# Regrouping in a fused GFNet mixing and SoLU kernel: one quarter of each transfer becomes a ScalarE copy

## The chip, the cores and the metric

The kernel runs on one core of a Trainium2 chip, in fp32. The metric is the device time of one execution in microseconds (us), as the median of several runs. The core's engines are named as in the profile: PE is TensorE (matmuls; PEld is its weight loads), DVE is VectorE, ACT is ScalarE, POOL is GpSimd, and SP is the engine that only issues transfers. "ACTq" and "SPq" mark work of an engine's sequencer, such as issuing a DMA.

## The reference

```python
def _attn_ref(x, filt_r, filt_i):            # x: 8 x 3136 x 256
    X = np.fft.rfft(x, axis=1)
    F = (filt_r + 1j * filt_i)[None, :, :]
    y = np.fft.irfft(X * F, n=x.shape[1], axis=1)
    return y.astype(np.float32)

def _moe_ref(x, w_in, w_out, g_ln):          # x: 25088 tokens x 256, d_ff 1024
    h = x @ w_in
    e = np.exp(h - np.max(h, axis=-1, keepdims=True))
    sm = e / (np.sum(e, axis=-1, keepdims=True) + 1e-09)
    solu = h * sm
    mu = np.mean(solu, axis=-1, keepdims=True)
    var = np.mean((solu - mu) ** 2, axis=-1, keepdims=True)
    ln = (solu - mu) / np.sqrt(var + 1e-06) * g_ln
    return ln @ w_out
```

The output of the first, with batch and sequence joined, is the input of the second.

## The kernel before, in words

The Fourier part works on one batch element after the other, as matmuls with tables (`first`, `forward`, `multiply`, `inverse`, `back_halves`), with intermediate results in DRAM (`d1`, `d2`). Its result lies in `y`, with channels on partitions, for two elements at a time. Element 0 is done ahead of the main loop; the others are spread over the main loop by the table `PLAN`.

The main loop is `step(k)`, for 196 blocks of 128 tokens and nine more steps (`LAG = 9`). An even step and the odd one after it (pair `j = k // 2`) belong together. Nothing is reordered afterwards: the kernel is recorded under a manual schedule, so the order in which `step` calls its helpers is the order of instructions on every engine.

For one pair of blocks, in the order of the data:
- `product(j, m)` (L867 to L876, matmuls `m<-w_in_sb,...`): the product with `w_in` for a pair of blocks in seven half-size products instead of eight (Strassen's form, Winograd's variant). Products 1, 6, 5 and 3 build up in one PSUM bank; `keep` (L896) copies what the bank holds by then to `h` on ScalarE, and `finish` (L907, L910) adds another bank on VectorE and takes the running minimum `nmax`. Product 3 adds to the bank which the `keep` behind product 5 reads, so it comes after that `keep`.
- `exponential` (L920, ScalarE), `normalize` (L932, VectorE: `h * e`) and `square` (L940, ScalarE, for the variance).
- `turn` (L950, VectorE): a transpose in blocks of 32 x 32. Four blocks of tokens share one `turn` tile `[128, 32, 4, 32]`. Its partition `32 a + j` holds features `32 f + j` of the tokens `32 a` to `32 a + 31` of each block.
- `regroup(p, i)` (L953 to L967): makes from one quarter `a = 2 * (p % 2) + i` of the turned tile the tile `solu_t`, in which all 128 partitions hold features. Partitions `32 a` to `32 a + 31` are read, and for each `q` of 0 to 3 the features with `f % 4 == q` go to the partitions `32 q` to `32 q + 31`: 32 partitions x 8 runs of 128 elements, 128 KB. Both calls of a pair stand in the even step, and their transfers are issued by SP. In the very last pairs a few are issued by ACT and POOL.
- `project_sums` (POOL, L854) and `project(p, m)` (L1022, matmuls `o<-w_out_sb,...`): the product with `w_out`, again in seven half-size products; `keep_out` (L1038, ScalarE) and `finish_out` (L1042, VectorE) join them into `ot` and scale by the token's `rs_t`, and `store_out` writes `ot`.

In an even step ScalarE's order around the change is: `keep_out` (L1038); in every other pair the copy of `rs_t` (L989); loads that belong to the Fourier part where there are any (`spectrum_loads`, L320 `t<-d` and L835 `de<-de_tbl`, issued on ACT's queue); then, in the odd step, `keep` behind product 5 (L896), `keep_out`, `exponential`, `keep_out`, `square`. TensorE's order there is: `project(p, 3)`, `project(p, 4)`, products 7 and 5, `project` 1 and 2, products 3 and 4, `project` 6 and 7.

`solu_t` has two buffers for each `i`; the tile of pair `p` takes the buffer of pair `p - 2`.

Of the kernel before, what the change touches and what calls it, by code (L numbers as in the profile page):

```python
# [110 lines left out]
def kernel(  # L111
# [10 lines left out]
    nc = tc.nc  # L122
# [356 lines left out]
    with ExitStack() as st:  # L479
# [140 lines left out]
        for i, h in [(i, h) for i in range(pieces - 2) for h in range(2)] + [  # L620
# [6 lines left out]
                           in_=ps.rearrange("p (a t c) -> p a t c", t=2, c=P))  # L627
# [36 lines left out]
        for i0, n, rows in ((0, 4, P), (4, 4, P), (8, NP - 9, P), (NP - 1, 1, NQ)):  # L664
            f, at = filters[i0]
            nc.sync.dma_start(
                out=f_dram[i0:i0 + n].rearrange("i u q k c -> (u q) i (k c)")[0:rows],
                in_=f[0:rows, at:at + n].rearrange("p i k c -> p i (k c)"))
# [163 lines left out]
    def load_de(sp, u, dma=nc.scalar.dma_start):  # L832
# [6 lines left out]
    turns, variances, solu_ts, solu_sums, spreads, rss, pos, ots, places, regrouped = (  # L839
        {} for _ in range(10))  # L840
# [112 lines left out]
    def regroup(p, i, dma=nc.sync.dma_start, parts=range(4)):  # L953


        g, second = divmod(p, 2)
        turned = turns[g].rearrange("p (k q) b i -> p k q (b i)", q=4)
        a = 2 * second + i
        if (p, i) not in regrouped:
            if p == last[-1]:  # L960
                st = pools["r"].tile([P, KF, P], FP32, name=f"solu_t_{p}_{i}", tag="r")
            else:
                st = upool.tile([P, KF, P], FP32, name=f"solu_t_{p}_{i}", tag=f"solu_t{i}")
            regrouped[p, i] = st
            solu_ts[p, i] = st[:, 0:KF // 2, :], st[:, KF // 2:KF, :]
        for q in parts:
            dma(out=regrouped[p, i][32 * q:32 * q + 32, :, :], in_=turned[32 * a:32 * a + 32, :, q, :])  # L967

    def least_variance(g):

# [95 lines left out]
    for e in range(1, B):  # L1066
# [5 lines left out]
        for i, t in enumerate(first_at):  # L1072
            if e == 1 and i < EARLY:
                continue
            dma = nc.gpsimd.dma_start
# [23 lines left out]
        for i, t in enumerate(spectrum_at):  # L1099
# [4 lines left out]
            dma = nc.sync.dma_start if e == 1 and t < 8 else nc.scalar.dma_start  # L1104
# [41 lines left out]
    def step(k):  # L1146
# [33 lines left out]
        if not odd:  # L1180
# [41 lines left out]
            if 0 <= j - 3 < pairs - 2:  # L1222
                regroup(j - 3, 0)
                regroup(j - 3, 1)
            elif j - 3 == pairs - 2:
                regroup(j - 3, 1, nc.scalar.dma_start, range(2))
                regroup(j - 3, 0)
                regroup(j - 3, 1, parts=range(2, 4))
                regroup(j - 2, 0)
                regroup(j - 2, 1, parts=range(2))  # L1230
# [107 lines left out]
```

## Time and profile before

| | us |
|---|---|
| median of 3 runs | 1560.1 (1558.52 to 1560.6) |
| profiled execution | 1558.44 |
| its span | 1556.7 |
| PE busy in the span | 1534.5 |
| DVE, POOL, ACT busy | 1241.3, 1107.3, 923.3 |
| granted clock of TensorE | 0.997 |

Times in the profile's rows are from the span's start. Matmuls overlap their weight loads, and their ends are modelled. A number in brackets behind a row of the timeline is the engine's idle time ahead of it and what ended it. Until about 1160 us the Fourier part runs among the token blocks; after that there are token blocks alone.

### The profile page before, as it was taken

The page shows a single profiled execution, that of the slowest core. Times are in us where ns is not written, and L with a number is a line of the kernel's source. Part 1 is how long each engine was busy: PE and PEld are TensorE (multiplying, and loading weights), DVE is VectorE, ACT ScalarE, POOL GpSimd, SP SyncE. Part 2 cuts the span into 40 slices and gives each one's busy share as a digit, 9 for nine tenths or more (in the row PEclk, how much of TensorE's full clock was granted, in tenths as well). Part 3 has the DMA queues.
Part 4 walks back from the last instruction along what each step waited for, and adds up shares of the span by engine and source line. Part 5 has one row for each costly group of instructions (what it writes and reads, how often), then busy time and mean ns, then how long its engine had stood idle before and what let it go on. Part 6 is the DMA issues. An engine that isn't in the chain of part 4 may idle for free. (4 is left out here: it accounts for less than half of the span.)

```text
span 1556.7 us, 36704 instructions
## 1 busy us (share of the span) xinstructions
PE 1534.5 (99%) x12922; PEld 1066.0 (68%) x12922; DVE 1241.3 (80%) x2220; ACT 923.3 (59%) x1893; POOL 1107.3 (71%) x1290
## 2 busy tenths in 40 slices
PE   9999999999999999999999999999999999999997
PEld 6735676666666776667666776667676777777777
DVE  5888878988988798868897699877987777777772
ACT  4556565665556565665656555665656656666662
POOL 2226776797879776986689678996767766676665
PEclk9999999999999999999999999999999999999999
DMA  9779587867986788667886678766874544344444
GB/s 250 267 254 274 160 229 218 238 196 212 245 242 188 188 247 238 198 164 202 248 230 183 166 209 246 209 181 185 228 206 118 135 122 121 97 119 105 107 109 109
DMA packets 340831, 297.58 MB, mean 191 GB/s; under 512 B 27313, under 2 KB 310731, under 8 KB 340649
## 3 DMA queue, kind: packets, MB, share of 16 engines
q1 hardware_dynamic: 277864, 175.33, 42.4%
q0 software_dynamic: 29152, 87.33, 18.7%
q10 hardware_dynamic: 33634, 32.58, 7.1%
q8 instruction: 105, 1.72, 0.5%
q14 instruction: 76, 0.62, 0.1%
HBM read 117.53 MB, written 74.84 MB: 124 GB/s over the span
## 5 line engine op out<-in xcount | busy, mean ns | idle before, releaser
L1022 PEld LDWEIGHTS o<-w_out_sb,solu_t 128*128 128x128 f32 x3136 | 381.7, 192 | 49.9 <-issue 43.1
L1022 PE MATMUL o<-w_out_sb,solu_t 128*128 128x128 f32 x3136 | 401.3, 276 | 3.7 <-DVE ot L1042 3.1
L1022 PEld LDWEIGHTS o<-w_out_sb,u 128*128 128x128 f32 x2352 | 307.3, 192 | 138.3 <-issue 108.6
L875 PE MATMUL m<-w_in_sb,s 128*128 128x512 f32 x760 | 384.5, 607 | 2.4 <-ACT h L896 1.6
L1022 PE MATMUL o<-w_out_sb,u 128*128 128x128 f32 x2352 | 310.7, 276 | 2.3 <-POOL u L854 1.8
L932 DVE SCALAR_TENSOR_TENSOR h<-e,h 128x1024 f32<-128x1024 f32 x196 | 304.5, 1554 | 0.0
L875 PE MATMUL m<-w_in_sb,y 128*128 128x512 f32 x570 | 297.1, 603 | 1.7 <-DVE h L907 1.2
L1038 ACT ACTIVATE ot<-o,rs_t 128x128 f32<-128x128 f32 x392 | 143.2, 367 | 244.6 <-PE o L1022 242.8
L896 ACT COPY h<-m 128x512 f32<-128x512 f32 x285 | 167.7, 588 | 200.5 <-PE m L875 179.7
L854 POOL TENSOR_TENSOR u<-solu_t 128x512 f32<-128x512 f32 x98 | 135.2, 1380 | 186.7 <-DMA solu_t<-turn 131.0
L910 DVE CUSTOM_DVE_ANT_0 h<-m,h 128x512 f32<-128x512 f32 x190 | 130.1, 685 | 166.8 <-ACT h L896 104.0
L940 ACT ACTIVATE h<-h,nmu 128x1024 f32<-128x1024 f32 x196 | 224.9, 1147 | 41.8 <-DVE turn L950 41.7
L950 DVE STREAM_TRANSPOSE turn<-h 128x1024 f32<-128x1024 f32 x196 | 243.2, 1241 | 3.2
L920 ACT ACTIVATE e<-h,nmax 128x1024 f32<-128x1024 f32 x196 | 225.3, 1149 | 9.3 <-DVE h L932 7.9
L854 POOL TENSOR_TENSOR u<-solu_t,u 128x512 f32<-128x512 f32 x98 | 136.9, 1396 | 99.6 <-PE o L1022 99.3
L1042 DVE SCALAR_TENSOR_TENSOR ot<-o,rs_t,ot 128x128 f32<-128x128 f32 x299 | 103.8, 347 | 100.1 <-ACT ot L1038 61.4
L875 PEld LDWEIGHTS m<-w_in_sb,s 128*128 128x128 f32 x760 | 124.5, 191 | 80.3 <-issue 63.0
L854 POOL TENSOR_TENSOR u<-u,solu_t 128x512 f32<-128x512 f32 x98 | 162.6, 1659 | 16.8 <-PE o L1022 7.6
L854 POOL TENSOR_TENSOR solu_t<-solu_t,solu_t 128x512 f32<-128x512 f32 x98 | 155.6, 1587 | 0.9
L875 PEld LDWEIGHTS m<-w_in_sb,y 128*128 128x128 f32 x570 | 93.6, 190 | 89.6 <-issue 45.9
L854 POOL TENSOR_TENSOR s<-y 128x128 f32<-128x128 f32 x190 | 94.4, 497 | 0.5
L437 PEld LDWEIGHTS py<-wb_t,t 50*64 50x64 f32 x3584 | 57.6, 134 | 42.9 <-issue 19.4
(153 smaller groups left out, 1939.0 us busy)
## 6 DMA issues: line engine op xcount, KB each, us to landing
solu_t<-turn SPq DMA_DIRECT2D x780, 128.0 KB
out_dram<-ot SPq DMA_DIRECT2D x196, 128.0 KB
t<-d POOLq DMA_DIRECT2D x112, 200.0 KB, 6.7
t<-d ACTq DMA_DIRECT2D x37, 512.0 KB
f<-f_dram POOLq DMA_DIRECT2D x37, 512.0 KB, 7.9
d<-g POOLq DMA_DIRECT2D x36, 512.0 KB, 4.8
d<-x POOLq DMA_DIRECT2D x80, 200.0 KB, 5.2
de<-de_tbl ACTq DMA_DIRECT2D x37, 256.0 KB
```

Of the source, the lines that this page charges most:

```text
L437: nc.tensor.matmul(out=views[g][64 * h:64 * h + 64, cb, i, :], lhsT=t4[rows, i, c0:c0 + 64], rhs=wb_t[rows, 0:N1], start=True, stop=True)
L854: nc.gpsimd.tensor_tensor(out=out, in0=in0, in1=in1, op=op)
L875: nc.tensor.matmul(out=ms[j, bank], lhsT=lhsT, rhs=w_in_sb[:, w, :], start=m in (1, 2, 7), stop=True, skip_group_check=True)
L896: nc.scalar.copy(out=h_half(k, i), in_=ms[j, 0])
L910: nc.vector.tensor_tensor_reduce(out=h_half(k, i), in0=ms[j, bank], in1=h_half(*kept), scale=1.0, scalar=sofar, op0=ALU.add, op1=ALU.min, ...
L920: nc.scalar.activation(out=e, in_=hs[k], func=AFT.Exp, bias=nmaxs.pop(k)[:, 1:2], scale=-1.0, accum_out=esums[g][:, i:i + 1])
L932: nc.vector.scalar_tensor_tensor(out=solu, in0=e, scalar=SHRINK, in1=solu, op0=ALU.mult, op1=ALU.mult, accum_out=nmu)
L940: nc.scalar.activation(out=solu, in_=solu, func=AFT.Square, bias=nmu, scale=-float(DFF), accum_out=variances[g][:, i:i + 1])
L950: nc.vector.transpose(out=turns[g][:, :, i, :], in_=solus[k].rearrange("p (f j) -> p f j", j=32))
L1022: nc.tensor.matmul(out=pos[p, bank], lhsT=lhs[:, f, :], rhs=w[:, f, :], start=f == 0 and (m in (1, 2, 7) or alone), stop=True, skip_group_ ...
L1038: nc.scalar.activation(out=out_half(p, *to)[0], in_=pos[p, 0], func=AFT.Copy, scale=rs)
L1042: nc.vector.scalar_tensor_tensor(out=ot, in0=pos[p, bank], scalar=rs, in1=out_half(p, *kept)[0], op0=ALU.mult, op1=ALU.add)
```

## The change

In `regroup`, where the quarter `q` that a transfer fills lies on the same partitions as the quarter `a` that it reads, ScalarE copies it from `turned` to `solu_t`; the other three remain transfers on the queue that issued them before. This holds for each of the 196 calls, in which exactly one `q` equals `a`. The copy takes the transfer's place in the program's order.

```diff
         for q in parts:
-            dma(out=regrouped[p, i][32 * q:32 * q + 32, :, :], in_=turned[32 * a:32 * a + 32, :, q, :])
+            move = nc.scalar.copy if q == a else dma
+            move(out=regrouped[p, i][32 * q:32 * q + 32, :, :], in_=turned[32 * a:32 * a + 32, :, q, :])
```

## The prediction

> **What bounds the kernel now.** I read the page first, then busy time by stage, then the timeline of single rounds, then the rows of the tile that the change touches. A round is one even step together with the odd step after it; it handles two blocks of 128 tokens; from the fourth round on each has a pair of `regroup` calls, 98 pairs in all. First the page's engine line:
>
> ```profile
> PE 1534.5 (99%) x12922; PEld 1066.0 (68%) x12922; DVE 1241.3 (80%) x2220; ACT 923.3 (59%) x1893; POOL 1107.3 (71%) x1290
> ```
>
> Then the windows of the first half and the middle (with Fourier work), of the late stage (without) and of the tail:
>
> ```profile
> 135.00:500.00 365.00, 360.09 (x3248) 244.84 (x3247) 313.90 (x537) 217.10 (x446) 284.09 (x333) 1.00 0.78 219
> 500.00:1160.00 660.00, 658.41 (x6096) 457.68 (x6095) 549.44 (x984) 402.55 (x828) 511.36 (x602) 1.00 0.75 208
> 1160.00:1510.00 350.00, 350.00 (x2471) 253.39 (x2470) 258.18 (x488) 216.24 (x446) 243.20 (x278) 1.00 0.44 115
> 1510.00:1557.00 47.00, 37.95 (x290) 35.00 (x288) 17.09 (x36) 15.89 (x38) 25.99 (x23) 0.92 0.45 118
> ```
>
> The columns are window, length, then PE, PEld, DVE, ACT and POOL busy, granted clock, DMA share and GB/s. TensorE is never idle in the late stage and 1.6 us in the middle, so it sets the end. A transfer or an engine matters only where it makes TensorE late. From 135 to 500 us TensorE idles 365 - 360.09 = 4.9 us. That and the tail are all there is to gain.
>
> What the quarter transfers cost now, from the rows of the tile `solu_t`:
>
> ```profile
> L967 SPq DMA_DIRECT2D solu_t<-turn x780: 585/625/3257, 118.4 to 1535.9; - x195
> ...
>   POOL u L854: 131.0, 42
>   ACT ot L1038: 33.8, 90
> ...
>   PEld o L1022: 2.2, 2
>   PE o L1022: 2.1, 2
> ```
>
> The first line is the issue time on SP (least, median, most, in ns), the others who waited on the tile. Mostly GpSimd waits, which has time to spare; TensorE hardly at all.
>
> **The change, part by part.** Removed: 196 of 784 transfers, 196 x 128 KB = 25.7 of 297.6 MB, and 196 x 0.625 = 122 us of SP issue time. SP computes nothing, and the matmuls read the regrouped tile a round later, so the gain is between 0 and the 4.9 us above with some of the tail; I take 2 us, as most of the 4.9 stands at other waits.
>
> Added: 196 ScalarE copies, 32 partitions x 1024 elements, SBUF to SBUF. No such row exists. The nearest are a PSUM copy over 512 elements per partition and SBUF passes over 1024 (busy us, mean ns of one, idle time before):
>
> ```profile
> L896 ACT COPY h<-m 128x512 f32<-128x512 f32 x285 | 167.7, 588 | 200.5 <-PE m L875 179.7
> ...
> L940 ACT ACTIVATE h<-h,nmu 128x1024 f32<-128x1024 f32 x196 | 224.9, 1147 | 41.8 <-DVE turn L950 41.7
> ```
>
> In these rows the time follows elements per partition: 559 ns for 512 more. Fewer partitions do not shorten it where that can be seen: copies of 100x512 (L250) took 0.58 to 0.60 us in the same stage as 0.58 to 0.60 for 128x512. So I take 32 partitions x 1024 as a pass over 1024. An L940 pass ends 1.15 us after it starts, but its successor starts 1.05 to 1.06 us after it. So a pair of copies holds ScalarE for 0.04 + 2 x 1.06 = 2.15 us. Bounds: below, 1.10 us a pair (a quarter of the partitions halves the time, the 0.53 us of a 512 copy); above, 2.5 us (VectorE's 1.24 us for 1024 elements). Below nothing is out, since a pass takes time on an engine that had none of it. ScalarE goes from 923 to about 923 + 196 x 1.06 = 1131 us, 73% of the span; it does not become the bound as a whole. What counts is the place.
>
> The Trainium skill (ScalarE: Activation LUTs, Rules for kernel authors) budgets about 0.3 us plus 0.83 ns an element, so 2.3 us a pair; by that my sum would be some 10 us more. The 1147 ns row agrees with it for one pass; the overlap of neighbours is what it leaves out.
>
> Where the pair stands: in program order behind the even step's `keep_out`, the `rs_t` copy and the ACT-queue loads of `t` and `de`, ahead of the next odd step's `keep` (the `h` copy of product 5, L896). Both slots' earlier readers, TensorE and GpSimd, and the turn are done by then, so the copies themselves wait for little. But `keep` queues behind them, and behind `keep` come `ot` (L1038) and the exponential; product 3 on TensorE waits for `keep`, the bank's reader. A round with loads and `rs_t`:
>
> ```profile
> 703.95 0.16 ACT L989 COPY rs_t<-o 128x4 f32<-128x4 f32 x1 [0.46 <-PE o L986]
> 704.11 0.39 ACTq L320 DMA_DIRECT2D t<-d  x1
> ...
> 704.53 0.70 ACTq L835 DMA_DIRECT2D de<-de_tbl  x1
> ...
> 705.77 0.58 ACT L896 COPY h<-m 128x512 f32<-128x512 f32 x1 [1.66 <-PE m L875]
> ...
> 706.71 0.37 ACT L1038 ACTIVATE ot<-o,rs_t 128x128 f32<-128x128 f32 x1 [0.35 <-PE o L1022]
> ...
> 707.24 0.30 PEld L875 LDWEIGHTS m<-w_in_sb,s 128*128 128x128 f32 x2
> ```
>
> ScalarE is free from 705.23 to 705.77, 0.54 us, since the issues stand ahead of the copies. `keep` becomes 2.15 - 0.54 = 1.61 us late. It ends at 706.35 now; product 3 loads its weights at 707.24, 0.89 us later, of which 0.05 is the signal: 0.84 us of slack. TensorE stalls 1.61 - 0.84 = 0.77 us. Afterwards ScalarE idles about 2 us ahead of its next `ot` (1.96 at 710.16), so it is back on time; the stall stays, as TensorE has no idle time to give back.
>
> The same round without loads, in the late stage:
>
> ```profile
> 1347.99 0.16 ACT L989 COPY rs_t<-o 128x4 f32<-128x4 f32 x1 [0.24 <-PE o L986]
> ...
> 1349.81 0.58 ACT L896 COPY h<-m 128x512 f32<-128x512 f32 x1 [1.66 <-PE m L875]
> ...
> 1350.75 0.37 ACT L1038 ACTIVATE ot<-o,rs_t 128x128 f32<-128x128 f32 x1 [0.35 <-PE o L1022]
> ...
> 1351.28 0.30 PEld L875 LDWEIGHTS m<-w_in_sb,s 128*128 128x128 f32 x2
> ...
> 1358.25 0.98 PEld L1022 LDWEIGHTS o<-w_out_sb,u 128*128 128x128 f32 x8 [0.55 <-ACT ot L1038]
> ```
>
> Here the gap is 1.66, `keep` is 0.49 late, and product 3 is not delayed. But `ot` had waited only 0.35, so it slips 0.14; VectorE's work runs on from `ot` with no break, the next exponential follows VectorE, and the last line shows TensorE already waiting for the `ot` behind it. So 0.14 us may pass through.
>
> I read gap and slack this way in 90 rounds of the timeline:
> - `rs_t` and loads, 23 rounds: 16 stall, 12.5 us together (gaps 0.30 to 0.67, 0.78 on average); 6 more, where the load's own wait ends last and the gap is 0.04, stall 1.4 to 2.1 us, 10.0 together; one has 2.16 of slack and hides it.
> - loads without `rs_t`, 17 rounds: the gap is mostly 1.4 to 1.6 and the slack covers the rest; three with less stall 2.5 us together.
> - no loads, 50 rounds: gaps 1.66 to 2.25, product 3 always covered; 13 late rounds with `rs_t` x 0.14 = 1.8 us.
>
> Sum of these: 26.8 us. Outside them lie four rounds from 118 to 170 us and two in which a copy of `t<-py` stands between (near 236 and 447 us); there ScalarE has about 1 us less room than it needs: 6 x 1 = 6 us. For the 14 covered rounds with loads whose `ot` slips 0.2 to 0.3 I take 1 us of a possible 4.
>
> The tail: four copies in a row stand behind the last block's square (its pass starts at 1526.64) and ahead of an `ot` that starts at 1528.50 and holds TensorE at 1529.01. They make it 4 x 1.06 less the 0.6 us idle there, 3.7 us, late. TensorE's later wait of 1.76 us on GpSimd's `u` at 1538.18 absorbs part, leaving 2.0; the two copies of the round before cost some 0.5: 2.5 us. SP's two fewer transfers there (1.25 us of issue) help only GpSimd's `u`.
>
> Total: 26.8 + 6 + 1 + 2.5 = 36.3, less the 2 us: 34 us. The profiled execution took 1558.4 us around its span of 1556.7; the median of the runs is 1560.1, 1.7 above. 1558.4 + 34 = 1592.4 for such an execution, about 1593 as a median: 2.1% slower.
>
> **The rivals.** *The copies hide (chance 0.10).* If 32 partitions are cheaper, 1.10 us a pair, only 7 rounds stall, 4.2 us, and the rest shrinks to 1 or 2: 1560 to 1568. Against it: nothing in the trace shows a ScalarE pass that is shorter for fewer partitions.
>
> *Faster (0.05).* With the copies hidden, lighter queues bring loads earlier in the DMA-heavy half (share 0.75 and more), where six rounds have `keep` waiting for the issue of `t`. The most is the 4.9 us of idle time plus 1 or 2 of the tail: 1552 to 1557. It needs the pair to take under some 1.1 us, or those loads to come over 2 us earlier. The Trainium skill (SBUF — State Buffer, Who interferes with whom) says that DMA never contends with a compute engine, so that the removed quarter gave the engines nothing back; the 2.1 us of TensorE's waits on the tile agree.
>
> *ScalarE and VectorE become the loop (0.17).* If a pair takes 2.5 us, 59 rounds stall, 34.7 us; late rounds pass on 9.7 through `ot`; covered rounds with loads up to 5; early rounds and tail 10: 59 us, 1618. It decides from about 2.3 us a pair. For it: VectorE is 80% busy and some of its 1.22 us passes take 2.27.
>
> That the change is not what it says is no rival: the changed program's order of instructions holds 196 copies, each pair ahead of the `keep`.
>
> **How the numbers follow.** The forecast (0.68) spans 1572 to 1610. The range, 1563 to 1620, reaches down into the hidden case and up to the loop's 1618 and a little past it; about 2 in 10 stays out. 0.2%, 3 us, is about what a measurement of this kernel can tell from no change. Faster takes the 0.05; the hidden case leaves 0.04 within 3 us; the rest is slower, 0.91.
>
> **What would show it.** Right: copies near 1.1 us; the `h` copy's idle time (200.5 us) mostly gone; TensorE waiting on ACT `h` or on `nmax`, about 0.8 us in rounds with loads; the middle longer by some 20 us, the late stage by about 2. Wrong: copies of half that; a late stage longer by over 10 us, which is the loop; or a round with loads as long as before.

## The result, and the profile after

The changed kernel took 1588.0 us as the median of 6 runs (1583.8 to 1589.8), the kernel before in the same sessions 1561.6: 26.5 us more, a ratio of 1.0165 with a 95% interval of 1.0145 to 1.0185. 1593 had been forecast, 2.1% above. The profiled execution of the changed kernel took 1583.8 us around a span of 1581.8, 25.1 us above the span before; it is the fastest of the six, and the rows below are of it.

From the page of the changed kernel: busy time, the SP and ACT queues' transfers (packets, MB, share of 16 engines' time), and two of the costliest groups (busy time, mean ns of one, idle time ahead and what ended most of it).

```profile
PE 1539.3 (97%) x12922; PEld 1068.1 (68%) x12922; DVE 1225.6 (77%) x2220; ACT 1126.3 (71%) x2089; POOL 1103.6 (70%) x1289
...
q1 hardware_dynamic: 225096, 149.89, 34.9%
...
L968 ACT COPY solu_t<-turn 32x1024 f32<-32x1024 f32 x196 | 204.0, 1041 | 53.1 <-issue 31.5
...
L896 ACT COPY h<-m 128x512 f32<-128x512 f32 x285 | 168.0, 590 | 29.9 <-PE m L875 23.0
```

The 196 copies are there, 1.041 us each; ScalarE is no bound at 71%. The idle time ahead of the `h` copies was 200.5 us and is 29.9: that is the gap into which the pairs went. The queue's share fell from 42.4% to 34.9%.

The windows show where the time went (columns as in the prediction), and the waits of TensorE between 190 and 1510 us what it waited for (us in total, times, longest):

```profile
135.00:500.00 365.00, 352.79 (x3190) 239.44 (x3189) 293.31 (x525) 257.99 (x480) 275.66 (x324) 1.00 0.70 199
500.00:1160.00 660.00, 649.79 (x5888) 450.90 (x5887) 529.79 (x961) 482.46 (x897) 501.38 (x595) 1.00 0.65 186
1160.00:1510.00 350.00, 349.53 (x2610) 252.40 (x2609) 264.52 (x492) 271.99 (x499) 243.22 (x280) 1.00 0.38 101
```

```profile
PE m L875 <- ACT h L896: 12.2, 20, 1.1
PE m L875 <- POOL s L854: 2.4, 4, 0.6
```

TensorE now idles 10.2 us in the middle window, where it idled 1.6, and from 190 to 1510 us it waits mostly for the `h` copy (1.6 us once before). The idle time in these rows is less than the time lost: in the round below the matmul's row shows 0.75 us of idle time where the row of its weight load shows 0.91. So I also compared the start of each round's first `turn` with that of before, by the times of before. At 207 us the changed kernel is 5.3 us behind, at 1193 us 22.2, at 1513 us 21.9, and at the end 25.1. Between 207 and 1193 us, 27 rounds lose 25.7 us and 12 win back 8.6 (changes of less than 0.25 us left out); from there to 1513 us no round loses or wins more than 0.5.

A round with loads, the same as in the prediction:

```profile
716.43 0.39 ACTq L320 DMA_DIRECT2D t<-d  x1
...
716.86 0.70 ACTq L835 DMA_DIRECT2D de<-de_tbl  x1
...
717.73 2.11 ACT L968 COPY solu_t<-turn 32x1024 f32<-32x1024 f32 x2 [1.30 <-issue]
...
719.87 0.59 ACT L896 COPY h<-m 128x512 f32<-128x512 f32 x1
...
720.56 0.30 PEld L875 LDWEIGHTS m<-w_in_sb,s 128*128 128x128 f32 x2 [0.91 <-issue]
720.60 1.10 PE L875 MATMUL m<-w_in_sb,s 128*128 128x512 f32 x2 [0.75 <-ACT h L896]
```

The pair starts 0.17 us after the end of the issue of `de` and holds ScalarE until the `h` copy; product 3's weights follow 0.10 us after the copy, 0.91 us later than they could. In a late round without loads there is no such wait:

```profile
1370.26 2.11 ACT L968 COPY solu_t<-turn 32x1024 f32<-32x1024 f32 x2
...
1372.39 0.59 ACT L896 COPY h<-m 128x512 f32<-128x512 f32 x1
1373.01 0.37 ACT L1039 ACTIVATE ot<-o,rs_t 128x128 f32<-128x128 f32 x1
...
1373.37 0.30 PEld L875 LDWEIGHTS m<-w_in_sb,s 128*128 128x128 f32 x2
...
1373.74 0.35 DVE L1043 SCALAR_TENSOR_TENSOR ot<-o,rs_t,ot 128x128 f32<-128x128 f32 x1
```

And the tail, where four copies in a row stand ahead of an `ot`, and TensorE waits for it:

```profile
1551.06 4.23 ACT L968 COPY solu_t<-turn 32x1024 f32<-32x1024 f32 x4
...
1555.31 0.37 ACT L1039 ACTIVATE ot<-o,rs_t 128x128 f32<-128x128 f32 x1
...
1555.82 2.05 PE L1023 MATMUL o<-w_out_sb,u 128*128 128x128 f32 x8 [4.21 <-ACT ot L1039]
```

### The profile page after: what moved, and what is told of

Same layout as the page of the kernel before. It is cut to its first block, busy times and chain, and to the rows that moved or that the text cites. A ratio compares the mean times of both kernels' runs of the same rounds, so it can differ in the third digit from the quotient of the medians.

```text
span 1581.8 us, 36704 instructions
## 1 busy us (share of the span) xinstructions
PE 1539.3 (97%) x12922; PEld 1068.1 (68%) x12922; DVE 1225.6 (77%) x2220; ACT 1126.3 (71%) x2089; POOL 1103.6 (70%) x1289
## 3 DMA queue, kind: packets, MB, share of 16 engines
q1 hardware_dynamic: 225096, 149.89, 34.9%
## 4 chain that ended last, share of the span: by engine, by line
PE 86%; DMA 5%; DVE 3%; ACT 2%; issue 2%; SPq 1%; POOL 1%; ACTq 0%; DVEq 0%; POOLq 0%
PE o L1023 35%; PE m L875 35%; PE py L437 4%; PE pb L330 3%; DMA solu_t<-turn 3%; PE pc L330 2%; PE pa L297 2%; PE pa L248 1%; ACT solu_t L968 1%; PE py L460 1%; DMA f<-in_filt_r_dram 1%; DMA d<-x 1%; PE d L882 1%; DVE turn L950 1%; ACT h L896 1%
## 5 line engine op out<-in xcount | busy, mean ns | idle before, releaser
L875 PE MATMUL m<-w_in_sb,s 128*128 128x512 f32 x760 | 386.6, 610 | 15.1 <-ACT h L896 12.2
L940 ACT ACTIVATE h<-h,nmu 128x1024 f32<-128x1024 f32 x196 | 224.9, 1147 | 40.5 <-DVE turn L950 40.5
L968 ACT COPY solu_t<-turn 32x1024 f32<-32x1024 f32 x196 | 204.0, 1041 | 53.1 <-issue 31.5
L854 POOL TENSOR_TENSOR u<-solu_t,u 128x512 f32<-128x512 f32 x98 | 133.6, 1363 | 141.6 <-PE o L1023 141.4
L896 ACT COPY h<-m 128x512 f32<-128x512 f32 x285 | 168.0, 590 | 29.9 <-PE m L875 23.0
L854 POOL TENSOR_TENSOR solu_t<-solu_t,solu_t 128x512 f32<-128x512 f32 x98 | 161.9, 1652 | 0.9
```

Source lines behind the costliest of these rows:

```text
L854: nc.gpsimd.tensor_tensor(out=out, in0=in0, in1=in1, op=op)
L875: nc.tensor.matmul(out=ms[j, bank], lhsT=lhsT, rhs=w_in_sb[:, w, :], start=m in (1, 2, 7), stop=True, skip_group_check=True)
L896: nc.scalar.copy(out=h_half(k, i), in_=ms[j, 0])
L940: nc.scalar.activation(out=solu, in_=solu, func=AFT.Square, bias=nmu, scale=-float(DFF), accum_out=variances[g][:, i:i + 1])
L968: move(out=regrouped[p, i][32 * q:32 * q + 32, :, :], in_=turned[32 * a:32 * a + 32, :, q, :])
```

## The experiments

Theory A: the loss is one of place. The pair holds up the `keep` behind it, and most where loads stand ahead of it. Theory B: it is ScalarE's total load, so much a copy. Theory C: regrouping by three transfers is itself later.

**The copies put off** (`e1_put_off`) to the odd step, behind the exponential:

```diff
-            move = nc.scalar.copy if q == a else dma
-            move(out=..., in_=...)
+            if q == a: put_off.append(ends)
+            else: dma(out=ends[0], in_=ends[1])
...
                 exponential(k - 2)
+            copies()          # nc.scalar.copy for all in put_off
```

> Both copies of a round are recorded later: not in the even step, ahead of the next keep, but in the odd step behind the exponential, where ScalarE idled about 2.0 us before. Copies, transfers and their number stay. Theory A (place: the pair holds up the keep behind it, most where loads stand ahead of it): the pair of 2.15 us fits the idle time nearly, so the middle loses nothing; four copies in a row in the tail still cost 2 to 3 us: 1560 to 1566 us. Theory B (ScalarE's total load, 0.135 us a copy wherever it stands): about 1588. Theory C (the regrouping by three transfers is itself later or out of order): about 1588.

Measured: 1555.9 us; the ratio to the kernel before is 0.9974 (0.9960 to 0.9988). All 196 copies are made, and the kernel is faster than before. B and C fall: they said 1588. A said that the loss would go, but 1560 to 1566 was too high, since I had counted no gain.

**The loads behind the pair** (`e2_loads_behind`):

```diff
-            for job in spectrum_loads[k]:
-                job()
             ... regroup calls ...
+            for job in spectrum_loads[k]:
+                job()
             if 0 <= j - 4 < pairs:
```

> As the changed kernel, but the Fourier part's loads on ScalarE's queue stand behind the pair of copies instead of ahead of it. Theory A: every round then has the gap of 1.66 us or more, so the stalls of the middle (17 us in the trace) fall to 0 to 4; early rounds (5 us) and tail (3 us) stay: 1566 to 1574 us. Theory B: 1588. Theory C: 1588.

Measured: 1557.2 us, 0.9987 (0.9975 to 0.9998). The copies are where the change put them, and the loss is gone; again the forecast was too high, by some 9 us at its lower end. The kernel before with its loads in the new place was not tried, so what the new place of the loads is worth without copies is open. ScalarE in a round with loads (702 us):

```profile
701.98 1.04 ACT L968 COPY solu_t<-turn 32x1024 f32<-32x1024 f32 x1
702.22 0.38 ACTq L320 DMA_DIRECT2D t<-d  x1
702.63 0.56 ACTq L835 DMA_DIRECT2D de<-de_tbl  x1
703.05 1.04 ACT L968 COPY solu_t<-turn 32x1024 f32<-32x1024 f32 x1
704.12 0.59 ACT L896 COPY h<-m 128x512 f32<-128x512 f32 x1
```

The loads are issued while the engine copies. In the changed kernel's order, the engine idled while they were issued (1.30 us at 717.73), and then copied: what costs is the sum of issue and pair ahead of `keep`.

**The copies on top** (`e3_copies_on_top`): all four transfers as before, and in the change's place copies into a tile that nobody reads.

```diff
             dma(out=regrouped[p, i][32 * q:32 * q + 32, :, :], in_=...)
+            if q == a:
+                for n in range(2):
+                    waste = wk.tile([P, 4, P], mybir.dt.uint8, ..., tag="waste")
+                    nc.scalar.copy(out=waste[32 * q:32 * q + 32], in_=turned[32 * a:32 * a + 32, 4 * n:4 * n + 4, q, :])
```

> All four transfers of the kernel before are kept, and ScalarE copies the quarter in addition, in the place of the changed kernel, into a waste tile that nobody reads (in two halves of 512 elements, as 8-bit numbers, for lack of room); the result is that of the kernel before. Theory A: the loss of the changed kernel, and a little more, since no transfer is saved: 1588 to 1600 us. Theory B: the same. Theory C: 1560 to 1564, since the regrouping is that of before.

Measured: 1614.5 us, 1.0354 (1.0329 to 1.0380). With the transfers untouched the loss is there, and twice as large: C is out for good. My size was wrong. Each half took 0.615 us and the two pairs of halves 2.55 us where the real pair takes 2.11:

```profile
735.01 2.55 ACT L971 CAST waste<-turn 32x512 uint8<-32x512 f32 x4 [1.76 <-issue]
737.59 0.59 ACT L896 COPY h<-m 128x512 f32<-128x512 f32 x1
```

From the end of the issue of `de` to the start of the `h` copy this makes 2.62 us, in each of the 40 rounds with loads that I read. With the gaps and slacks of the kernel before, read as in the prediction, 2.62 us gives 41.5 us of stalls, against 25.0 for 2.15. The other 13 us were not taken apart: by the starts of `turn` this kernel is 7.9 us behind at 189 us, where the changed one is 5.0, and it loses 5.0 more in the tail. In the waits of TensorE between 190 and 1510 us the `h` copy has risen from 12.2 to 28.5:

```profile
PE m L875 <- ACT h L896: 28.5, 24, 2.6
```

**One copy of two** (`e4_one_of_two`): only the first `regroup` call of a round copies.

```diff
-            move = nc.scalar.copy if q == a else dma
+            move = nc.scalar.copy if q == a and i == 0 else dma
```

> Only the first of a round's two regroup calls copies; the other keeps four transfers. Theory A: one copy and its start take about 1.25 us, less than gap plus slack in all but the rounds where the gap is 0.04; my table of gaps gives 5 us there, early rounds and tail 2 or 3: 1564 to 1570. Theory B: half the loss, about 1575. Theory C: half the loss or more, about 1575.

Measured: 1558.8 us, 0.9992 (0.9976 to 1.0007): half of the copies cost nothing that can be measured, not half of the loss. So the cost is not so much a copy, as B has it. The 5 us of stalls that the gaps gave are not seen; half of the gain from saved transfers (below) would about cover them, which was not tried by itself.

**Put off, and the tail by transfers** (`e5_put_off_no_tail`): as `e1_put_off`, with

```diff
+            if q == a and p not in last:     # last: the final five pairs
```

> The copies put off to the odd step as in e1_put_off, and in the last five pairs all four quarters by transfers, as in the kernel before. If e1's gain over the kernel before (4 us) comes from fewer transfers in the DMA-heavy half, it stays and the tail's loss of 1 to 2 us goes: 1553 to 1556 us. If e1's gain came from the tail, this is at 1560.

Measured: 1552.2 us, 0.9956 (0.9944 to 0.9968). It beats both kernels. Its windows: TensorE is busy all of the middle, and 362.13 us of the first 365 where it was 360.09 before.

```profile
135.00:500.00 365.00, 362.13 (x3254) 245.97 (x3255) 306.73 (x543) 265.64 (x496) 286.66 (x336) 1.00 0.71 204
500.00:1160.00 660.00, 660.00 (x6111) 460.17 (x6110) 545.96 (x986) 490.50 (x913) 511.04 (x604) 1.00 0.66 190
1160.00:1510.00 350.00, 350.00 (x2470) 253.80 (x2469) 260.24 (x489) 268.52 (x498) 247.07 (x275) 1.00 0.36 96
```

**Put off, on top of four transfers** (`e6_put_off_on_top`): the waste copies of `e3_copies_on_top`, on 128 partitions and in the place of `e5_put_off_no_tail`.

```diff
+                waste = wk.tile([P, 4, P], mybir.dt.uint8, name="waste", tag="waste")
+                nc.scalar.copy(out=waste, in_=whence[:, 4 * n:4 * n + 4, :])
```

> All four transfers as in the kernel before, and in the place of e1_put_off ScalarE in addition copies the quarter to a waste tile that nobody reads, on all 128 partitions instead of 32 and in two halves of 512 elements as 8-bit numbers; not in the last five pairs. The result is that of the kernel before. If e1's gain comes from the transfers that it saves, nothing is gained here: 1559 to 1565 us (the pair is some 0.4 us longer than e1's). If it comes from anything else, 1556. If the time of a copy goes by partitions, these take more than the 0.615 us that the same halves took on 32 partitions in e3_copies_on_top; if by elements per partition, the same.

Measured: 1559.7 us, 0.9999 (0.9983 to 1.0014). So copies in this place are free, even longer ones, and the 0.44% that `e5_put_off_no_tail` gains (7.5 us between the two medians) belong to the saved transfers. The halves took the same on 128 partitions as on 32 (0.615 us in `e3_copies_on_top`); the row of their tile:

```profile
L959 ACT CAST waste<-turn x372: 602/618/652, 126.5 to 1490.4; 128x512 uint8<-128x512 f32 x186
```

One way in which fewer transfers can save time stands in the traces. A VectorE pass of the Fourier part (L355) precedes an `ot` here, and TensorE waits for that `ot`. First the kernel before, then `e5_put_off_no_tail`:

```profile
783.61 3.33 DVE L355 TENSOR_TENSOR pr<-pr,pt 128x512 f32<-128x512 f32 x1
783.88 1.27 POOL L854 TENSOR_TENSOR solu_t<-solu_t,solu_t 128x512 f32<-128x512 f32 x1
785.11 1.27 POOL L854 TENSOR_TENSOR u<-solu_t,u 128x512 f32<-128x512 f32 x1
786.86 0.34 DVE L1042 SCALAR_TENSOR_TENSOR ot<-o,rs_t,ot 128x128 f32<-128x128 f32 x1
...
787.25 0.38 PE L1022 MATMUL o<-w_out_sb,solu_t 128*128 128x128 f32 x1 [1.04 <-DVE ot L1042]
```

```profile
780.41 1.28 POOL L854 TENSOR_TENSOR solu_t<-solu_t,solu_t 128x512 f32<-128x512 f32 x1
781.16 2.31 DVE L355 TENSOR_TENSOR pr<-pr,pt 128x512 f32<-128x512 f32 x1
781.64 1.26 POOL L854 TENSOR_TENSOR u<-solu_t,u 128x512 f32<-128x512 f32 x1
783.39 0.34 DVE L1053 SCALAR_TENSOR_TENSOR ot<-o,rs_t,ot 128x128 f32<-128x128 f32 x1
```

In the kernel before, GpSimd's two passes over `solu_t` lie within the VectorE pass. With fewer transfers they start earlier against it, and the VectorE pass is 1 us shorter. GpSimd's chain of that round begins with a pass that starts at 777.70, after 5.81 us of waiting for the regrouping transfers, and with fewer transfers at 774.52. In `e6_put_off_on_top`, with all four transfers, it takes 3.34 us again and TensorE waits 1.52. From 190 to 1510 us TensorE waits 2.3 us for VectorE's `ot` in the kernel before, 1.8 in `e6_put_off_on_top`, and not at all in `e5_put_off_no_tail`. That would be a part of the 7.5 us; no run isolates it.

**The tail alone** (`e7_no_tail`): the changed kernel with `q == a and p not in last`.

> The changed kernel, with all four transfers in the last five pairs, as in the kernel before. The four copies in a row ahead of an ot copy are gone, on which TensorE waited 4.21 us in the changed kernel's trace. Theory A: 2.5 to 3.5 us less than the changed kernel, 1584 to 1586. If the tail's end is set by the transfers anyway: 1588.

Measured: 1582.3 us, 1.0137 (1.0114 to 1.0160), against 1.0165 for the change. The two intervals overlap, so the medians alone do not show the tail's cost. The traces do: from 1513 us to the end the changed kernel loses 3.2 us against the kernel before, and this one wins 0.4. TensorE's wait of 4.21 us for `ot` is gone, and the old waits for POOL's sums and the transfers stand there again (waits of TensorE from 1530 us):

```profile
PE o L1023 <- POOL u L854: 1.7, 1, 1.7
PE o L1023 <- DMA solu_t<-turn: 1.3, 1, 1.3
```

**Only the rounds without loads** (`e8_free_rounds`), 96 copies in the change's place:

```diff
+            move = nc.scalar.copy if q == a and p not in last and not spectrum_loads[2 * p + 6] else dma
```

> The changed kernel's copies, in its place, but only in the 48 rounds without the Fourier part's loads and not in the last five pairs: 96 copies instead of 196, the others by transfers. Theory A (place: without loads the gap of 1.66 us or more and the slack cover the pair): 1557 to 1562 us. Theory B (0.135 us a copy wherever it stands): 1560 + 96 x 0.135 = 1573.

Measured: 1561.8 us, 1.0003 (0.9984 to 1.0022): free within the interval, as A said, and well below B's 1573. What its fewer transfers gained is not known, and could hide a cost of a few us. Its runs spread widely (1555.9 to 1569.6) and the profiled one is the slowest, so its trace is not read.

**Two variants of the best.** `e9_loads_behind_no_tail` is `e2_loads_behind` with transfers in the last five pairs; `e10_no_ends` is `e5_put_off_no_tail` with transfers in the first four pairs too.

> The copies in the changed kernel's place, with the Fourier part's loads behind them (as e2_loads_behind), and all four transfers in the last five pairs. In e2's trace the main loop ended 4 us ahead of the kernel before and the tail gave 1 to 3 back; without that: 1552 to 1556 us. If the place still costs something in the rounds without loads (gap 1.66 against a pair of 2.15), it is slower than e5_put_off_no_tail (1552) by a few us.

> As e5_put_off_no_tail, with all four transfers in the first four pairs as well, where its trace was 1.7 us behind the kernel before by 208 us. If the copies cause that, 1550 to 1552 us, ahead of e5; if it is the run's own variation, as e5: 1552.

Measured: 1555.2 us, 0.9968 (0.9956 to 0.9981), and 1554.2 us, 0.9957 (0.9941 to 0.9973). The second is `e5_put_off_no_tail` over again (0.9956): copies in the first four pairs cost nothing that can be measured. The intervals of `e9_loads_behind_no_tail` and `e5_put_off_no_tail` overlap, so whether the odd step is the better place is open; that both beat the kernel before is not.

## Why the prediction was right

The direction and the mechanism were right: the pair in front of `keep`, stalls in rounds with loads, a wait in the tail. The size was 7.5 us too high (34 forecast, 26.5 measured). The two terms furthest off are the six rounds of the load's own wait and the gain, both on the same side; the smaller errors go both ways and partly cancel, which is luck. A round's stall is read here as the idle time ahead of product 3's weight load. By the prediction's steps:

- *The copy's price.* 2.12 us a pair by the neighbours' spacing; measured 2.11. That 32 partitions cost as much as 128 is shown by the halves above. The Trainium skill (ScalarE: Activation LUTs, Rules for kernel authors) budgets 0.3 us plus 0.83 ns an element, by estimate 1.15 us, for a pass with a bias operand. The 1147 ns row has one and agrees; this copy has none and took 1.041.
- *Rounds with loads and `rs_t`.* 12.5 us was forecast for 16 rounds; in the changed kernel the same 16 stall 12.2 us. The round shown, with 0.91, is one of the longest. There 2.31 us pass from the issue of `de` to `keep`, where the prediction has 2.15; in the 40 rounds with loads that I read it is 2.16 to 2.31, in the median 2.18, since the pair starts 0.04 us after the issue in 23 of them.
- *Rounds with loads, without `rs_t`.* 2.5 us was forecast for 17 rounds, and 4.2 came.
- *Six rounds with the load's own wait, 10 us.* Here the forecast went wrong. These six rounds stalled 3.1 us together, since the issues that had waited did not wait again in them: from the start of `t` to the end of `de` they took 0.84 to 1.22 us, where they had taken 1.66 to 3.09. The kernel before shows one:

```profile
428.05 0.38 ACTq L320 DMA_DIRECT2D t<-d  x1
430.77 0.37 ACTq L835 DMA_DIRECT2D de<-de_tbl  x1
431.18 0.58 ACT L896 COPY h<-m 128x512 f32<-128x512 f32 x1 [4.25 <-DMA x<-in_x_dram]
```

  Between the two issues ScalarE's queue waits 2.3 us, by the profile until an earlier transfer (`x<-in_x_dram`) has landed, and `keep` stands behind. In that round TensorE already waited 1.57 us for the `h` copy before the change. Such waits move from run to run: 8 of 44 load pairs took over 1.6 us before and 4 in the changed kernel, three of them in other rounds. So to take each of the six as it stood in one trace was the mistake.
- *The gain, 2 us, with 4.9 and some of the tail as the most.* It is some 7, shown by `e5_put_off_no_tail` against `e6_put_off_on_top`. How it comes about is open. Shorter issue waits alone do not explain it: `e5_put_off_no_tail` has 3 pairs over 1.6 us, but `e10_no_ends`, just as fast, has 5, and so has `e6_put_off_on_top`, which gains nothing. The shorter VectorE passes shown above are a second way.
- *Late rounds, 1.8 us through `ot`.* Nothing was lost. `ot` slipped by about 0.17 us, but VectorE's `ot` (1373.74) starts as long after TensorE's group as before (2.04 us). In the kernel before, VectorE's `ot` of such a round starts at 1351.65 with ACT `ot` in its bracket, but ACT `ot` had ended at 1351.12 and TensorE's group at 1351.56: TensorE ended that wait.
- *Six rounds with less room, 6 us, and the tail, 2.5.* By 207 us, with four of the six, 5.3 us are lost; of the other two the one near 236 us loses 1.4 and the one near 447 us nothing. The tail loses 3.2.
- *The rivals.* The hidden copies did not come true in this place, but do in another. The ScalarE and VectorE loop did not close: the late stage lost nothing. Faster was given 0.05 and needs a place that hides the pair; with one the kernel is 0.44% faster. The Trainium skill (SBUF — State Buffer, Who interferes with whom) says that DMA never contends with a compute engine. No run here contradicts it, but it was wrong to conclude from it that fewer transfers give the engines nothing back: an engine's queue waits for transfers too, and a transfer's landing sets when another engine's passes run.

## What to carry to other kernels

On an in-order engine a new instruction is priced by the gap at its place, less what the queue has to issue ahead of it, plus the slack of whoever waits for the instruction behind it; the engine's total busy time says little about it. Here 196 copies in the place of transfers cost 26.5 us in one place, and the kernel became 4 us faster when they were recorded in the odd step instead, where the engine had idled about 2 us. With the tail left to transfers it was some 7 us faster. Before work is moved to an engine, find the gap in its order; and when transfers are saved, look who issues other transfers between compute instructions, and whose passes start by their landing.

## What the runs showed of the hardware

- A ScalarE copy from SBUF to SBUF took 1.041 us for 1024 fp32 elements on 32 partitions, and a cast of 512 elements 0.615 and 0.618 us on 32 and 128 partitions: here the number of partitions made no difference.
- DMA issues on ScalarE's queue run beside its engine when they stand behind an instruction that is already running (702.22 us inside a copy that ends at 703.02), but an instruction behind them starts only after them, 0.04 to 0.17 us after the last issue in the changed kernel (0.17 at 717.73).
- An issue can itself wait, by the profile for an earlier transfer's landing (2.3 us at 428 us in the kernel before), and the `keep` recorded behind it on that engine waited with it.
- A VectorE pass over two 128x512 fp32 tiles (L355) took 3.33 us with two GpSimd passes of 1.27 us beside it (783.61 in the kernel before) and 0.69 with no GpSimd pass beside it (445.93). Why it is so is not shown here.
